# Threshold attention into a SwiGLU feed-forward: long score bursts from step 48, one last group of four chunks, and a feed-forward paced over 16 steps

## The chip, the cores and the metric

The kernel runs on one core of one Trainium2 chip. The metric is the device time of one execution in microseconds (us). Shown of the kernel before are four such times and one profiled execution. Engine names: PE is TensorE, DVE is VectorE, ACT is ScalarE, POOL is GpSimd, SP is SyncE, which here only issues DMAs.

## The reference, cut to what matters

Eight batches of eight heads, 576 positions, head width 64. Attention keeps only the scores within `tau` of the row's largest one; the result is the input of a gated feed-forward over 4608 rows of width 512, inner width 1536.

```python
scores = q @ k.T / 8
scores = where(scores >= max(scores, -1) - tau, scores, -1e9)
attn = exp(scores - max) / sum
x = (attn @ v) laid out as [8 * 576, 512]
xn = x / sqrt(mean(x * x) + 1e-6) * rms_g
out = (silu(xn @ w_gate) * (xn @ w_val)) @ w_out
```

## The kernel before

**Tiling.** The 4608 rows are 36 chunks of 128 rows: four main chunks for each batch, and one chunk (kind "v") for each pair of batches that holds their last 64 rows. A chunk takes four steps, one for each pair of heads, so there are 144 steps. In step s, PE computes 128 x 576 scores in fp32 for each of two heads into the two score tiles `s_ps` (two PSUM banks each; `emit_burst`, matmuls on L581). DVE moves them to `ssb` and takes the row extreme in the same instruction (L614, "TTR" below, with a small read of the accumulator after each). POOL makes the threshold (L652), ACT and partly POOL mask and exponentiate (L663 to L701), a DMA transposes the weights (L730), and PE multiplies them with V every second step (L748 and L753, "AV"). When a chunk's four steps are through, `emit_x` normalizes its 512 columns and a DMA transposes them into `xnT` (L800).

**Bursts.** A burst is one uninterrupted run of score matmuls. Up to step SB a burst is one step, 576 columns for each head. From step SB on a burst is 1024 columns for each head, both banks full, whatever step they belong to (`plan_bursts`); a step's scores are then cut in pieces at the ends of bursts, and each piece has its own TTR. A burst may begin when all TTRs of the burst before it have read the score banks. If a burst touches a "v" chunk, all of it is made of 64 x 64 matmuls.

**Feed-forward.** Chunks are collected in groups (SIZES); a group's rows are the moving columns, 256 for two chunks and 512 for four. `emit_ffn` makes 12 slices of the inner width: four gate matmuls (L854), four value matmuls (L859), a tanh on ACT (L868), two operations on DVE (L871, L876). Then 12 output matmuls for each chunk (L924), in two halves (OUT_PART), a move out of PSUM to `osb` (L937 on DVE or L939 on ACT, chosen by OUT_DVE) and a store on SP's queue (L944). The last group is "streamed": its output matmuls (L899) follow its gates slice by slice into accumulators that stay open, the banks named by ACC, and its moves out alternate between DVE and ACT.

**Order.** Nothing is ordered by hand. Every operation has an engine, a planned cost, a priority in units of steps and the operations that it needs. `order_ops` simulates the engines and, on each engine, picks what can start first, and among those the lowest priority; the program is then issued in that order, and each engine runs its list in order. A group's first slice has as priority the step of its last chunk plus LAG, or the end of the group before it, whichever is later, and its 12 slices are spread over PACE steps for each 512 columns; with SPREAD the output matmuls of its chunks follow, spread over as many steps again. PART_PRIO draws an output's second half forward. A move out of PSUM and a tanh stand 40 steps ahead of their slice (PUSH), so they go as soon as their input is there. A TTR of step s has priority s - 1 + TTR_PRIO.

**PSUM.** Four banks are a ring for everything but scores. After the last TTR the banks in OPENS join the ring.

Of the kernel before, what the change touches and what calls it, by code (L numbers as in the profile page):

```python
# [15 lines left out]
COST = dict(  # L16
    s_main=965.0, s_virt=960.0, tr_qk=530.0, tr4=230.0, tr_full=440.0, av_main=290.0, av_virt=370.0, ffn4=215.0, warm=3500.0,
    evac_qk=600.0, evac_qk_act=465.0, evac_half=252.0, evac_kt=330.0, evac_kt_act=252.0, prelu=667.0, exp2=1060.0, exp1=666.0, exp0=590.0,
    mask_d=680.0, mask_g=1810.0, take_g=1360.0, trw=510.0, evac_w=400.0, evac_wp=900.0, rz=210.0, xmul=341.0, sq=612.0, xn=773.0,
    pool_tiny=302.0, pool_mean=944.0, pool_dma=880.0, cast_v=620.0, cast_vt=475.0, cast_w=665.0,  # L20
    sp=420.0, sp_v=600.0, sp_w=600.0, sp_tr=1300.0, sp_qk=680.0, sp_tl=630.0,
)
# [105 lines left out]
def kernel(  # L128
# [14 lines left out]
    NT, DM = out.shape  # L143
# [11 lines left out]
    def sb(name, shape, dt=FP32):  # L155
        return konst.tile(shape, dt, tag=name, name=name)
# [25 lines left out]
    ssb = [sb(f"ssb{i}", [128, 2, S]) for i in range(3)]  # L182
# [22 lines left out]
    hf = [sb(f"hf{i}", [128, 512], FP16) for i in range(12)]  # L205
    hf += [stg.bitcast(FP16)[:, 512 * i:512 * (i + 1)] for i in range(NHF - 12)]
    osb = [sb(f"osb{i}", [128, DM]) for i in range(2)]

    s_ps = [ps(f"s_ps{h}", 1024) for h in range(2)]
    ROW_AT = 512 - S // 2  # L210
# [12 lines left out]
    def add(eng, cost, prio, deps, fn, **kw):  # L223
        o = Op(eng, cost, prio, deps, fn, **kw)
        ops.append(o)
        return o
# [57 lines left out]
    o_id, o_c, o_v, o_g = setup()  # L284
# [258 lines left out]
    ttr_of, exp_of, wt_of, av_of = {}, {}, {}, {}  # L543
# [23 lines left out]
    def emit_burst(segs, prio, runs):  # L567

        info = {s: parts_of(s) for s, _, _, _ in segs}
        no_whole = any(w is None for _, w, _ in info.values())  # L570
        deps = [x for d, _, _ in info.values() for x in d] + last_ttr
        made = []
        for run in runs:
            def fn(o, run=run):
                for s, lo, hi, at in run:
                    _, whole, quads = info[s]
                    p = steps[s][1]
                    for rows, i, lhs in quads if no_whole or o.quad else whole:
                        for h in range(2):
                            hs = HALF[h]  # L580
                            nc.tensor.matmul(s_ps[h][rows, at:at + hi - lo], lhs(hs), kT[i][p][h][hs, lo:hi],  # L581
                                             start=True, stop=True)

            n = sum(hi - lo for _, lo, hi, _ in run)
            o = add("PE", COST["s_main"] * n / S if not no_whole else COST["s_virt"] * n / S, prio if not made else -600.0,
                    deps + made[-1:], fn, mode=2 if no_whole else 1)
            if not made and REL_N[0] <= prio < REL_N[1]:
                o.release = REL[0] + REL[1] * prio
            made.append(o)
        for s in info:  # L590
            ci, p = steps[s]
            kind, b, c = chunks[ci]
            s_of.setdefault(s, made[0])
            if kind == "m":
                last_s.setdefault(("k", b, p), [])
                last_s["k", b, p] = last_s["k", b, p] + made
            else:
                last_sv[b, p] = last_sv.get((b, p), []) + made
                for e in range(2):
                    last_s.setdefault(("k", 2 * b + e, p), [])  # L600
                    last_s["k", 2 * b + e, p] = last_s["k", 2 * b + e, p] + made
        last_ttr.clear()
        for s, lo, hi, at in segs:
            first, last = lo == 0, hi == S
            if first:
                buf = s % 3
                held = exp_of[ssb_user[buf]] if buf in ssb_user else []
                ssb_user[buf] = s
            else:
                held = []  # L610
            for h in range(2):
                def ttr(o, s=s, lo=lo, hi=hi, at=at, h=h, first=first, last=last):
                    m = s % 6
                    nc.vector.tensor_tensor_reduce(  # L614
                        out=ssb_of(s)[:, h, lo:hi], in0=s_ps[h][:, at:at + hi - lo], in1=zrow[:, lo:hi],
                        scale=-1.0 / 8.0, scalar=3.0e38 if first else mxp[m][:, h:h + 1], op0=ALU.add, op1=ALU.min,
                        accum_out=(mx if last else mxp)[m][:, h:h + 1])

                before = [] if first else [ttr_of[s, h]]
                t = ttr_of[s, h] = add("DVE", 75.0 + (hi - lo) / 0.96, s - 1 + TTR_PRIO, made + [o_c] + held + before, ttr)  # L620
                last_ttr.append(t)

    last_ttr = []
# [204 lines left out]
    count = dict(hf=0, gv=0, o=0, v=[])  # L828
    clock = [0.0]

    def emit_ffn(slot, parts, ready_step, pace, streamed):

        n = 128 * len(parts)
# [4 lines left out]
        clock[0] = st + pace * n / 512.0  # L838
        xops = [t for _, t in parts]
        hs = []  # L840
        mm = 4 * (COST["ffn4"] if n == 512 else 112.0 if n == 256 else 60.0)
        el = n / 0.96 + 65.0
        uses = []
        for fc in range(NFC):
# [4 lines left out]
            hi = count["hf"] % NHF  # L849
# [28 lines left out]
            t = add("ACT", n / 1.2 + 49.0, pr - PUSH[0], [g, th_use.get(i)], tanh)  # L878
# [8 lines left out]
        if streamed:  # L887
# [6 lines left out]
            for n_, (fc, js) in enumerate(turns):  # L894
                hi, m_ = hs[fc]
# [16 lines left out]
        for j, (ci, _) in enumerate(parts):  # L912
            kind, b, c = chunks[ci]
            pr = st + dt * (NFC + (j + OUT_AT) * (NFC / len(parts) if SPREAD and not streamed else 1.0))
            oi = count["o"] % 2
            count["o"] += 1
            if streamed:
                mo, at = acc, j
            else:
                mo, at = None, 0  # L920
                for lo in range(0, NFC, OUT_PART):
                    def omm(o, j=j, lo=lo, first=mo):
                        for fc in range(lo, lo + OUT_PART):
                            nc.tensor.matmul(ring[(first or o).slot[0]], hf[hs[fc][0]][:, 128 * j:128 * (j + 1)],  # L924
                                             wo[:, fc], start=(fc == 0), stop=(fc == NFC - 1))

                    need = [m_ for _, m_ in hs[0:lo + OUT_PART]] + wo_ld + (outs[-1:] if mo else [])
                    o = add("PE", OUT_PART * COST["ffn4"], pr - (0.0 if lo == 0 else PART_PRIO), need, omm, ring=None if mo else "R")
                    mo = mo or o
                    outs.append(o)  # L930

            late = streamed and j % 2
            on_dve = streamed and not late or not streamed and OUT_DVE[ci % len(OUT_DVE)]

            def ev(o, oi=oi, mo=mo, at=at, on_dve=on_dve):
                if on_dve:
                    nc.vector.tensor_scalar(out=osb[oi], in0=ring[mo.slot[at]], scalar1=0.5, scalar2=None, op0=ALU.mult)  # L937
                else:
                    nc.scalar.activation(out=osb[oi], in_=ring[mo.slot[at]], func=AF.Copy, scale=0.5)  # L939

            def store(o, oi=oi, kind=kind, b=b, c=c, late=late):
                if kind == "m":
                    dst = out[b * S:b * S + MAIN].rearrange("(si sc) d -> si sc d", sc=4)[:, c]
                    (nc.scalar if late else nc.sync).dma_start(out=dst, in_=osb[oi])  # L944
                else:
                    for e in range(2):
                        r0 = (2 * b + e) * S + MAIN
                        nc.sync.dma_start(out=out[r0:r0 + TAIL], in_=osb[oi][64 * e:64 * e + 64])

            e = add("DVE" if on_dve else "ACT", 600.0 if on_dve else 476.0, pr - PUSH[0],  # L950
                    [last_out[j] if streamed else outs[-1], osb_use.get(oi)], ev,
                    frees=(mo, at))
            late = late and kind == "m"
            osb_use[oi] = add("ACT" if late else "SP", COST["sp"] if kind == "m" else 1100.0, pr, [e], store,
                              dma=DMA_NS['out'])
# [25 lines left out]
    n = 0  # L981
    for c in range(DFF // 512):
        for d in range(0, 4, 2):
            for w_dram, w_sb in ((moe_w_gate, wg), (moe_w_val, wv)):
# [7 lines left out]
                lo = gated(add("SP", COST["sp_w"], pr, w_use[slot], load, dma=2 * DMA_NS['w'], bulk=True), pr)  # L992
# [21 lines left out]
    for s, (ci, p) in enumerate(steps):  # L1014
# [6 lines left out]
        if p == NP - 1:  # L1021
            gi, j = place[ci]
# [23 lines left out]
            o.fn(o)  # L1046


PACE = 13.0
SQ_DVE = (0,)  # L1050
OUT_DVE = (0,)
LAGS = ()
SB = 64
TTR_PRIO = 1.0
BY_ROW = 4
ACC = (4, 6)
OPENS = ((4,), (6,))
NHF = 24
SPREAD = True
OUT_AT = 0.0  # L1060
PART_PRIO = 1.0
SIZES = (2, 2, 2, 2, 4, 4, 4, 4, 4, 4, 2, 2)
LAG = 16.0
LAT_TR = 3000.0
LAT_LD = 2000.0
REL = (0.0, 0.0)
# [64 lines left out]
```

## Time and profile before

| | us |
|---|---|
| median of 4 runs | 551.6 |
| lowest and highest | 550.87, 552.32 |
| profiled execution, its time | 552.32 |
| profiled execution, its span | 550.5 |
| PE busy in the span | 541.6 |
| ACT busy | 451.1 |
| DVE busy | 434.0 |
| POOL busy | 322.5 |

The profiled execution is the slowest of the four; 1.8 us of its time lie outside the span. A profile's row of a group gives the line, the engine, the operation, the tiles out<-in, the shape, the count, then busy time in us and the mean of one in ns, then the idle time ahead of it and what ended it. PE's matmuls overlap in the records, so the distance from one block's start to the next block's start is what counts, and a block in which a matmul waits shows as a longer busy block.

### The profile page before, as it was taken

What the parts mean: (1) busy time and instruction counts of PE and PEld (TensorE: products, weight loads), DVE (VectorE), ACT (ScalarE), POOL (GpSimd) and SP (SyncE); (2) the same over time, 40 slices, a digit from 0 to 9 for tenths busy, and PEclk for the clock granted to TensorE, in tenths of its full rate; (3) what the DMA queues carried; (4) which work ended last, traced back from release to release, by engine and by line L of the source; (5) the groups of instructions that cost most, each with busy time, mean ns of one, the idle gap of its engine ahead of it and who ended that gap; (6) DMA issues with size and microseconds to landing.
All of it is one profiled execution on the core that took longest, in us unless ns stands there. A gap on an engine that the chain in (4) does not pass through costs nothing.

```text
span 550.5 us, 15126 instructions
## 1 busy us (share of the span) xinstructions
PE 541.6 (98%) x5664; PEld 313.8 (57%) x5664; DVE 434.0 (79%) x1251; ACT 451.1 (82%) x741; POOL 322.5 (59%) x462
## 2 busy tenths in 40 slices
PE   8999999999999999999999999999999999999997
PEld 4656666666667455545555556555655454455764
DVE  4898988888878688878896889798897889775633
ACT  5898889899988889788989899899899988863332
POOL 2367846886777666665758467667767665631000
PEclk9999999999999999999999999999999999999999
DMA  8999999879998688798998698989997664740111
GB/s 194 246 274 280 170 179 215 162 128 186 188 194 178 132 172 157 161 188 167 176 206 159 116 200 179 198 153 214 188 180 152 127 123 94 157 95 29 40 58 57
DMA packets 270025, 89.07 MB, mean 162 GB/s; under 512 B 252544, under 2 KB 262272, under 8 KB 269952
## 3 DMA queue, kind: packets, MB, share of 16 engines
q1 hardware_dynamic: 267168, 86.02, 79.5%
q0 software_dynamic: 1600, 1.57, 1.9%
q8 instruction: 44, 0.72, 0.5%
q10 hardware_dynamic: 1184, 0.52, 0.3%
q14 instruction: 29, 0.24, 0.1%
HBM read 37.75 MB, written 9.44 MB: 86 GB/s over the span
## 4 chain that ended last, share of the span: by engine, by line
PE 90%; ACT 3%; DMA 2%; POOL 2%; DVE 2%; issue 1%; SPq 0%; DVEq 0%
PE s_ps L581 26%; PE ring L854 16%; PE ring L859 16%; PE ring L924 15%; PE ring L753 6%; PE ring L306 2%; PE ring L748 2%; DVE ssb L614 1%; DMA stg<-in_moe_w_val_dram 1%; PE s_ps L859 1%; PE s_ps L854 1%; ACT ssb L663 1%; DMA stg<-in_moe_w_gate_dram 1%; PE s_ps L899 1%; PE s_ps L924 1%
## 5 line engine op out<-in xcount | busy, mean ns | idle before, releaser
L614 DVE CUSTOM_DVE_ANT_0 ssb<-s_ps,zrow 128x576 f32<-128x576 f32 (+8 forms) x288 | 182.1, 669 | 26.0 <-PE s_ps L581 21.8
L663 ACT ACTIVATE ssb<-ssb,nth 128x576 f32<-128x576 f32 x224 | 166.6, 767 | 22.5 <-POOL nth L652 22.1
L581 PE MATMUL s_ps<-qkt 64*64 64x288 f32 (+16 forms) x1688 | 158.8, 415 | 2.3 <-DVE mx L614 1.8
L696 POOL TENSOR_SCALAR wsb<-ssb,nth 128x576 f16<-128x576 f32 x64 | 110.5, 1727 | 9.4 <-DMA wt<-wsb 2.6
L581 PEld LDWEIGHTS s_ps<-qkt 64*64 64x64 f32 (+1 forms) x1688 | 77.0, 144 | 60.0 <-issue 19.4
L854 PE MATMUL ring<-xnT,wg 128*128 128x256 f16 (+1 forms) x536 | 109.7, 327 | 0.2 <-DVE wt L724 0.2
L859 PE MATMUL ring<-xnT,wv 128*128 128x256 f16 (+1 forms) x536 | 109.7, 327 | 0.0
L670 ACT ACTIVATE wsb<-ssb 128x1152 f16<-128x1152 f32 x80 | 92.8, 1160 | 1.1
L652 POOL TENSOR_SCALAR nth<-mx 128x2 f32<-128x2 f32 x144 | 31.7, 220 | 105.5 <-DVE mx L614 91.0
L871 DVE SCALAR_TENSOR_TENSOR sl<-th,ring 128x512 f32<-128x512 f32 (+1 forms) x134 | 73.6, 551 | 25.1 <-ACT th L868 24.5
L701 POOL TENSOR_TENSOR wsb<-wsb,esb 128x576 f16<-128x576 f16 x64 | 81.9, 1280 | 9.5 <-ACT esb L682 5.0
L868 ACT ACTIVATE th<-ring 128x512 f32<-128x512 f32 (+1 forms) x134 | 64.3, 481 | 21.8 <-PE ring L854 18.1
L859 PEld LDWEIGHTS <-wv 128*128 128x128 f16 x576 | 53.0, 98 | 42.0 <-issue 8.7
L854 PEld LDWEIGHTS <-wg 128*128 128x128 f16 x576 | 53.2, 98 | 39.9 <-issue 6.7
L614 DVE CUSTOM_DVE_ANT_0 ssb<-s_ps,zrow,mxp 128x128 f32<-128x128 f32 (+7 forms) x80 | 38.2, 515 | 24.4 <-PE s_ps L581 24.0
L682 ACT ACTIVATE esb<-ssb,nth 128x576 f16<-128x576 f32 x64 | 49.3, 770 | 7.8 <-POOL nth L652 7.7
L753 PE MATMUL ring<-va,wt 128*128 128x65 f16 (+1 forms) x1280 | 50.9, 193 | 0.0
L924 PE MATMUL ring<-wo,hf 128*128 128x512 f16 x204 | 48.4, 380 | 0.0
L753 PEld LDWEIGHTS <-wt 128*128 128x128 f16 (+1 forms) x1280 | 46.1, 100 | 3.0
L667 ACT ACTIVATE wsb<-ssb 128x576 f16<-128x576 f32 x64 | 43.5, 680 | 1.1
L924 PE MATMUL ring<-wo,stg 128*128 128x512 f16 x180 | 42.2, 379 | 0.0
L876 DVE TENSOR_TENSOR hf<-ring,sl 128x512 f16<-128x512 f32 (+1 forms) x68 | 38.3, 564 | 4.0
(71 smaller groups left out, 566.1 us busy)
## 6 DMA issues: line engine op xcount, KB each, us to landing
vst<-in_v_dram SPq DMA_DIRECT2D x32, 256.0 KB, 3.6
qkn<-in_k_dram SPq DMA_DIRECT2D x31, 256.0 KB, 4.4
out_dram<-osb SPq DMA_DIRECT2D x31, 256.0 KB, 2.7
qkn<-in_q_dram SPq DMA_DIRECT2D x28, 256.0 KB, 4.5
stg<-in_moe_w_gate_dram SPq DMA_DIRECT2D x6, 512.0 KB, 6.2
stg<-in_moe_w_val_dram SPq DMA_DIRECT2D x6, 512.0 KB, 6.6
wt<-wsb SPq DMA_TRANSPOSE x128, 3.4
wo<-in_moe_w_out_dram POOLq DMA_DIRECT2D x4, 384.0 KB, 6.7
```

Source lines behind the costliest of these rows:

```text
L581: nc.tensor.matmul(s_ps[h][rows, at:at + hi - lo], lhs(hs), kT[i][p][h][hs, lo:hi], start=True, stop=True)
L614: nc.vector.tensor_tensor_reduce(out=ssb_of(s)[:, h, lo:hi], in0=s_ps[h][:, at:at + hi - lo], in1=zrow[:, lo:hi], scale=-1.0 / 8.0, scalar ...
L663: nc.scalar.activation(out=sb_[:, h], in_=sb_[:, h], func=PRELU, scale=-1.0, bias=nth[m][:, h:h + 1], **PRELU_KW)
L670: nc.scalar.activation(out=wsb[s % NW], in_=sb_, func=AF.Exp)
L696: nc.gpsimd.tensor_scalar(out=wsb[s % NW][:, h], in0=sb_[:, h], scalar1=nth[m][:, h:h + 1], scalar2=None, op0=ALU.is_le)
L701: nc.gpsimd.tensor_tensor(out=wsb[s % NW][:, h], in0=wsb[s % NW][:, h], in1=esb[es], op=ALU.mult)
L753: nc.tensor.matmul(ring[o.slot[0]][rs, at:at + D + 1], w[:, 5 * h + j, rs], va[vi][:, p, 2 * j + h], start=False, stop=(h == 1 and j == 3))
L854: nc.tensor.matmul(ring[o.slot[0]][:, 0:n], wg[d][:, fs], xnT[slot][:, d, 0:n], start=(d == 0), stop=(d == 3))
L859: nc.tensor.matmul(ring[o.slot[0]][:, 0:n], wv[d][:, fs], xnT[slot][:, d, 0:n], start=(d == 0), stop=(d == 3))
L868: nc.scalar.activation(out=th[i][:, 0:n], in_=ring[g.slot[0]][:, 0:n], func=AF.Tanh, scale=0.5)
L871: nc.vector.scalar_tensor_tensor(out=sl[i][:, 0:n], in0=th[i][:, 0:n], scalar=1.0, in1=ring[g.slot[0]][:, 0:n], op0=ALU.add, op1=ALU.mult)
L924: nc.tensor.matmul(ring[(first or o).slot[0]], hf[hs[fc][0]][:, 128 * j:128 * (j + 1)], wo[:, fc], start=(fc == 0), stop=(fc == NFC - 1))
```

## The change

- SB goes from 64 to 48: 16 steps more are done in bursts of 1024 columns.
- TTR_PRIO goes from 1.0 to 0.0 for all steps (TTR_FROM is 0, so TTR_EARLY is not used).
- The last two groups of two chunks become one of four. It is the streamed one, its four accumulators are the four score banks, and all four open after the last TTR of their head. Its third and fourth chunk move to buffers that lie on `ssb` instead of `osb`.
- OUT_DVE goes from 0 to 1: the move out of PSUM of the groups that are not streamed goes from ACT to DVE.
- PACE goes from 13 to 16, LAG from 16 to 12, PART_PRIO from 1 to 2.
- The planner's cost of a gate slice of 256 columns goes from 112 to 113 ns for each matmul; 512 columns keep 215.

```diff
+    osb += [ssb[0][:, 0, 0:DM], ssb[0][:, 0, 0:DM], ssb[1][:, 0, 0:DM], ssb[2][:, 0, 0:DM]]
...
-                t = ttr_of[s, h] = add("DVE", 75.0 + (hi - lo) / 0.96, s - 1 + TTR_PRIO, made + [o_c] + held + before, ttr)
+                t = ttr_of[s, h] = add("DVE", 75.0 + (hi - lo) / 0.96, s - 1 + (TTR_PRIO if s >= TTR_FROM else TTR_EARLY), made + [o_c] + held + before, ttr)
...
-        mm = 4 * (COST["ffn4"] if n == 512 else 112.0 if n == 256 else 60.0)
+        mm = 4 * {512: 215.0, 384: 189.0, 256: 113.0, 128: 60.0}[n]
...
-            oi = count["o"] % 2
+            oi = 2 + j if streamed and j > 1 else count["o"] % 2
...
-PACE = 13.0
+PACE = 16.0
 SQ_DVE = (0,)
-OUT_DVE = (0,)
+OUT_DVE = (1,)
 LAGS = ()
-SB = 64
-TTR_PRIO = 1.0
+SB = 48
+TTR_PRIO = 0.0
+TTR_EARLY = 1.0
+TTR_FROM = 0
 BY_ROW = 4
-ACC = (4, 6)
-OPENS = ((4,), (6,))
+ACC = (4, 5, 6, 7)
+OPENS = ((4, 5), (6, 7))
...
-PART_PRIO = 1.0
-SIZES = (2, 2, 2, 2, 4, 4, 4, 4, 4, 4, 2, 2)
-LAG = 16.0
+PART_PRIO = 2.0
+SIZES = (2, 2, 2, 2, 4, 4, 4, 4, 4, 4, 4)
+LAG = 12.0
```

## The prediction

> **What bounds the kernel now.** I read the page first. PE is busy nearly all the span, and the chain that ended last runs through it.
>
> ```profile
> PE 541.6 (98%) x5664; PEld 313.8 (57%) x5664; DVE 434.0 (79%) x1251; ACT 451.1 (82%) x741; POOL 322.5 (59%) x462
> PE 90%; ACT 3%; DMA 2%; POOL 2%; DVE 2%; issue 1%; SPq 0%; DVEq 0%
> ```
>
> A busy PE may hide waits, so next come the stages (columns: window, its length, then busy us of PE, weight loads, DVE, ACT, POOL, each with its count).
>
> ```profile
> 60.00:160.00 100.00, 99.83 (x1235) 65.41 (x1235) 83.34 (x237) 90.81 (x161) 71.35 (x98) 1.00 1.02 177
> 160.00:220.00 60.00, 60.00 (x657) 34.15 (x655) 49.16 (x127) 53.04 (x89) 38.53 (x55) 1.00 0.87 162
> 220.00:300.00 80.00, 79.67 (x798) 43.94 (x802) 65.84 (x202) 69.77 (x110) 53.17 (x71) 1.00 0.91 175
> 300.00:380.00 80.00, 80.00 (x847) 43.18 (x837) 67.92 (x209) 71.61 (x114) 52.83 (x73) 1.00 0.92 175
> 380.00:480.00 100.00, 100.00 (x1055) 52.13 (x1054) 84.03 (x264) 91.34 (x145) 68.53 (x93) 1.00 0.77 148
> ```
>
> From 60 to 480 us PE is full at a granted clock of 1.00, ACT is busy 376.6 of 420 us (89.7%) and DVE 350.3 (83.4%). Last I read the chain in order of time, start to start, for what a burst costs and where one waits.
>
> ```profile
> 144.91 1.57 PE s_ps L581 x16
> ...
> 148.92 1.13 PE s_ps L581 x16
> ...
> 154.09 1.80 PE s_ps L581 x16
> ...
> 225.79 1.89 PE s_ps L581 x32
> 227.68 0.97 PE ring L854 x4
> 228.65 0.86 PE ring L859 x4
> ```
>
> A short burst takes 1.13 us and a long one 1.89. The block next to a burst takes 0.97 where it otherwise takes 0.86: 0.11 for each burst. Blocks of 1.57 and 1.80 are short bursts that waited. In the PE timeline I found five such: at 55.9 (0.36 over), 59.3 (0.67), 144.8 (0.45), 154.0 (0.67) and, with transposes attached, 161.1 (0.67): 2.8 us. After 165 us every burst takes its plain time. So outside the first 60 us the change can take time only out of PE's own work, out of these 2.8 us, and out of the end.
>
> **The change, part by part.**
>
> *Long bursts from 48.* Sixteen steps are 16 short bursts, 16 x (1.13 + 0.11) = 19.8 us; in the long form 16 x 576 / 1024 = 9 bursts, 9 x (1.89 + 0.11) = 18.0. **Gain 1.8 us**, on PE, which is full there. DVE pays: 9 bursts cut 16 steps into 24 pieces, 16 TTRs more for two heads. A whole TTR is 753 ns; pieces of 448 and 128 columns are 620 + 349, and another accumulator read is 83: 0.3 us each, 4.8 us in all, beside PE's work. Steps 48 to 63 ran from 161 to 220 us, where DVE is busy 49 of 60. Without that cover it costs at most 4.8. That the "v" steps 52 to 55 now lie in long bursts costs nothing by the rows: long bursts with the later "v" steps also took 1.88 to 1.89.
>
> *One last group of four.* In the PE timeline four matmuls of 256 columns take 0.437 us and four of 512 columns 0.862. The two groups' 48 blocks of the first kind (21.0) become 24 of the second (20.7): **0.3 us** on PE. DVE saves 24 x (416 + 422) - 12 x (682 + 689) ns = 3.7 us, in the end phase, where it idles.
>
> *OUT_DVE.* The moves out of PSUM change engine.
>
> ```profile
> L939 ACT ACTIVATE osb<-ring 128x512 f32<-128x512 f32 x32 | 18.8, 588 | 15.1 <-PE ring L924 15.0
> ...
> 546.07 0.69 DVE L937 TENSOR_SCALAR osb<-s_ps 128x512 f32<-128x512 f32 x1 [0.80 <-PE s_ps L899]
> ```
>
> ACT had 35 of 36, DVE will have 34: ACT loses 33 x 0.59 = 19.5 us, DVE gains 33 x 0.69 = 22.8. Counted in the windows, 26 lie between 60 and 480 us: DVE there goes to 350.3 + 17.9 + 4.8 = 373 of 420 (88.8%), ACT to 376.6 - 15.3 = 361 (86.0%). The load is turned over, not raised beyond where ACT was. Behind a move on DVE stand TTRs, and PE's next burst waits for those; the move goes first by its priority. Cover: DVE sat idle 38.7 us between 80 and 480 waiting for a burst to end, so it usually had caught up; 22.7 us come off that, 16 stay. Cost between a gain (the TTR pair at 153.2 us started 1.54 us late, by the wait row because of ACT's `osb`, and the 1.80 burst follows) and 26 x 0.69 = 17.9 us. I take zero, the end next to the row: no burst after 165 us waited on an ACT as full as DVE will be.
>
> The Trainium skill speaks against this edit: "Advanced Engine Details and Errata", section on the read-write bubble, says that ScalarE is closer to PSUM and VectorE to SBUF, to be used accordingly. The two rows agree in direction, 0.59 against 0.69, and so by the rule the edit loses 3.3 us of engine time in 33 moves. By the stage table that is not time of the kernel, since neither engine is the one that is full.
>
> *TTR_PRIO.* TTRs go ahead of gate work that is due at the same time.
>
> ```profile
> 158.91 0.42 DVE L871 SCALAR_TENSOR_TENSOR sl<-th,ring 128x256 f32<-128x256 f32 x1 [0.90 <-ACT th L868]
> 159.43 0.42 DVE L876 TENSOR_TENSOR stg<-ring,sl 128x256 f16<-128x256 f32 x1
> 159.90 0.42 DVE L871 SCALAR_TENSOR_TENSOR sl<-th,ring 128x256 f32<-128x256 f32 x1
> 160.24 0.75 DVE L614 CUSTOM_DVE_ANT_0 ssb<-s_ps,zrow 128x576 f32<-128x576 f32 x1
> ```
>
> The burst at 157.84 ended at 158.97; its TTRs stood behind three gate operations, the first of which waited for ACT, until 160.24, and the burst at 161.05 waited 0.67. The others behave alike. All 2.8 us are of the kinds that this edit and the last act on. In return gate operations are later and hold ring banks longer. Gain between 2.8 us and a loss of the same size; **I take half, 1.4**, as a new order makes some waits of its own.
>
> *PACE, LAG, PART_PRIO.* The groups' work is moved, not changed. A group of four arrives every 16 steps; before, 13 steps of gates were followed by three without, now they are even. The first gate cannot come much sooner: the second `xnT` of the first group landed at 49.3 us and the first gate ran at 52.6. Stores on SP and moves on DVE go along with the outputs, in the same number. I take zero, between a gain of 3.3 us (all of that distance) and the seam below.
>
> *The seam.* Before, the last burst began at 478.1 and ended at 479.9; the last `xnT` landed at 500.9, 20.9 us later, and 27 us went by before PE used it, with other groups' work. Now the last group needs all its four chunks first. What else is left? Before, two of the next-to-last full group's slices were done when the last burst began, by due time a cut at step 145. The same cut leaves now: of the group due from 139, seven of 12 slices (7 x 1.72 = 12.1 us) and its outputs (4 x 2.59 = 10.4), two outputs of the one before it (5.2), and three AVs (1.8): 29.5 us against 20.9. **Nothing lost**, with 8.6 us to spare. At the very end, slices of 512 columns need 0.7 us more from gate to product (0.584 + 0.682 + 0.689 against 0.375 + 0.416 + 0.422), but outputs run about five slices behind, and the last move and store stay as they are.
>
> **Sum.** 1.8 + 0.3 + 1.4 = 3.5 us. The profiled execution took 552.3 (span 550.5 and 1.8 around it), which gives 548.8; it stands 0.7 above the median, so for the median of runs I say 551.6 - 3.5 = **548.1**.
>
> **Rivals.**
> 1. *DVE becomes late for the bursts* (slower). Place: 160 to 480 us, TTRs behind moves out of PSUM. For it: DVE at 88.8%, and the moves come first. Against it: 16 us of waiting for PE remain. It decides the sign once PE loses over 3.5 us, that is six bursts in 54 by 0.67 each. If every other of the 26 moves costs its 0.69, 9.0 us: 551.6 - 3.5 + 9.0 = 557.1; with a third 554.1.
> 2. *The last group starves PE at the seam* (slower). If PE runs ahead of its due times by six more steps (some 4 slices and an output, 9.5 us), the spare 8.6 is gone; each step further costs about 2 us. With three: 548.1 + 6 = 554.
> 3. *The gain is given back*: TTRs and moves trade waits, PE loses in new places the 1.4 and the 1.8; 551.6, that is, the change does not do what it is to do.
> 4. *More*: all five waits go (1.4 more), and the slices move up into the start by 1 us: 545.7.
>
> **How the numbers follow.** Forecast 0.57, with 546.5 to 550.4 about it; rival 4 0.11; rival 3 0.10; rival 1 0.13; rival 2 0.09. The bound for same is 0.2%, 1.1 us, about what a measurement of this kernel can tell from no change. Faster 0.57 + 0.11 = 0.68, same 0.10, slower 0.22. For 8 in 10 I take the forecast, rivals 3 and 4 and the near edge of the slower ones: 545.3 to 553.0.
>
> **What would show it.** Right: 54 bursts of 1.89 us and 48 short ones; 24 last blocks of 0.86; short bursts of 1.13 between 140 and 165 us or none there; PE full from the last burst to the last output; DVE near 89% and ACT near 86% in the loaded stretch. Wrong: long bursts over 1.9 us or PE idle ahead of them, released by DVE (rival 1); PE idle some 20 us after the last burst, released by `xnT` (rival 2). The prediction falls if the planner's new order lets DVE fall behind its plan, which I can't see in this trace.

## The result, and the profile after

The changed kernel takes 552.95 us (median of 38 runs, 551.36 to 554.78), the kernel before on the same chips 551.98 (60 runs, 550.69 to 554.15): ratio 1.0018, 95% interval 1.0012 to 1.0024. It is slower by about 1.0 us; I had forecast 3.5 us less than 551.6, that is 548.1. The four runs shown of before had their median 0.4 us under the one of the 60, so 0.4 us of the difference to my number is only that. Of all executions in this document one, of the rows kernel below, took 1361 us; it is left out of every number.

First the page of the profiled execution (time 551.96 us, span 550.2): engines, the chain by engine, and two groups of section 5.

```profile
PE 538.4 (98%) x5556; PEld 304.1 (55%) x5556; DVE 454.5 (83%) x1292; ACT 434.0 (79%) x696; POOL 322.1 (59%) x462
...
PE 86%; DMA 3%; DVE 3%; ACT 3%; POOL 2%; issue 1%; SPq 1%; ACTq 0%; POOLq 0%; DVEq 0%
...
L582 PE MATMUL s_ps<-qkt 64*64 64x288 f32 (+17 forms) x1676 | 155.8, 414 | 1.2 <-DVE mx L615 0.8
...
L855 PE MATMUL ring<-xnT,wg 128*128 128x512 f16 (+1 forms) x496 | 107.1, 338 | 1.6 <-DVE qkt L454 1.1
```

PE is busy 3.2 us less than before, near the 3.5 of the forecast, yet the span hardly moved, as PE is idle 2.9 us more; its share of the chain fell from 90% to 86%, and those of DVE and DMA rose from 2% to 3% each. The last column says for what PE sat idle. New there are the gate blocks (L855) that wait for a copy of DVE (L454). The row of the bursts (L582, 0.8 us on score reads) says nothing about the loaded stretch: its two waits lie at 32.8 and 41.4 us, and the five such waits of the kernel before (1.8 us) all lie in the first 51 us. For the loaded stretch the length of a burst tells, start to start; three lines of the chain of the kernel after, in order of time:

```profile
175.38 1.89 PE s_ps L582 x32
...
308.24 1.89 PE s_ps L582 x32
...
423.75 1.89 PE s_ps L582 x24
```

Of the 54 long bursts 53 take 1.82 to 1.95 us, as the 45 long ones of before do; one, at 168.6 us, takes 2.16, which is 0.3 more than its kind. The old waits at 144.8, 154.0 and 161.1 us are gone. So rival 1, bursts late because of DVE, didn't come. The stages of the kernel after, in the columns of the prediction's table:

```profile
60.00:160.00 100.00, 99.85 (x1227) 65.96 (x1225) 86.94 (x241) 88.00 (x156) 68.77 (x93) 1.00 1.01 176
160.00:220.00 60.00, 59.30 (x642) 34.51 (x640) 53.18 (x159) 51.22 (x85) 38.32 (x55) 1.00 0.84 160
220.00:300.00 80.00, 79.52 (x797) 43.22 (x794) 68.52 (x209) 67.29 (x104) 53.07 (x72) 1.00 0.94 181
300.00:380.00 80.00, 79.66 (x835) 42.77 (x834) 71.80 (x215) 69.59 (x109) 53.32 (x73) 1.00 0.90 167
380.00:480.00 100.00, 100.00 (x1054) 52.37 (x1051) 87.72 (x267) 85.78 (x134) 66.81 (x91) 1.00 0.79 142
```

DVE does 368.2 of 420 us (I had said 373) and ACT 361.9 (361). The granted clock is 1.00 as before. What I had not said is the third column: PE is no longer full from 160 to 380 us (59.30, 79.52 and 79.66 us, before 60.00, 79.67 and 80.00). The PE timeline shows where (start, duration, then the idle time before and what ended it):

```profile
208.96 0.22 PE L749 MATMUL ring<-va,wt 128*128 128x130 f16 x1
...
210.34 1.02 PE L855 MATMUL ring<-xnT,wg 128*128 128x512 f16 x4 [0.63 <-DVE qkt L454]
...
265.69 1.02 PE L855 MATMUL ring<-xnT,wg 128*128 128x512 f16 x4 [0.48 <-DVE qkt L454]
...
338.89 0.46 PE L307 MATMUL ring<-id,qkn 64*128 64x64 f32 x8 [0.34 <-DMA qkn<-in_q_dram]
...
542.95 1.89 PE L900 MATMUL s_ps<-wo,hf 128*128 128x512 f16 x8 [0.78 <-DVE osb L938]
545.62 0.81 PE L900 MATMUL s_ps<-wo,hf 128*128 128x512 f16 x3 [0.78 <-DVE ssb L938]
```

Two kinds matter. After an AV block, a gate block finds no free ring bank: the bank was still to be copied by DVE. And at the very end two of the streamed group's output rows wait for DVE's move out of the row before. The starts of neighbouring matmuls show the full price of such a wait: 0.95 us each at the end, 0.79 and 0.65 at 210 and 265.

**The account.** Both kernels stream the same number of columns in all, so I summed over the trace, for each matmul, the distance to the next start beyond its streaming time (0.42 ns a column of f16, by the blocks of 0.862 and 0.437 us in the prediction; 0.84 ns a column of f32 for the two or four matmuls that run side by side, by neighbouring starts in a burst), and set the two kernels against each other by which block follows which. From 80 us on the kernel after has +2.1 us among output blocks (the end), +2.0 from AVs to gate blocks (the ring: 0.79, 0.65 and, at 497.6 us, 0.35; the rest in small amounts), +0.7 among transposes (they wait for a load of `qkn`), and -3.0 in bursts and the blocks next to them: 1.8 us of old waits gone, and 1.2 because there are fewer changes into and out of bursts. That is +1.8. In two more profiles of the unchanged kernel after it is +2.1 and +2.4, in a second one of before 0.0. In the first 80 us the sum is 23.0 to 23.7 after and 24.2 and 25.3 before, some 1.4 less. Spans agree: 550.2, 550.8 and 551.4 after, 550.5 and 549.4 before, on the mean +0.8, beside +1.0 by the medians. The pair of profiles in the prediction and above happened to be a long execution of before and a short one of after.

### The profile page after: what moved, and what is told of

Its sections match the earlier page's. It is cut to its first block, busy times and chain, and to the rows that moved or that the text cites. A ratio compares the mean times of both kernels' runs of the same rounds, so it can differ in the third digit from the quotient of the medians.

```text
span 550.2 us, 14896 instructions
## 1 busy us (share of the span) xinstructions
PE 538.4 (98%) x5556; PEld 304.1 (55%) x5556; DVE 454.5 (83%) x1292; ACT 434.0 (79%) x696; POOL 322.1 (59%) x462
## 4 chain that ended last, share of the span: by engine, by line
PE 86%; DMA 3%; DVE 3%; ACT 3%; POOL 2%; issue 1%; SPq 1%; ACTq 0%; POOLq 0%; DVEq 0%
PE s_ps L582 26%; PE ring L855 16%; PE ring L860 16%; PE ring L925 13%; PE ring L754 5%; PE s_ps L900 2%; DVE ssb L615 2%; PE ring L307 2%; PE ring L749 2%; DMA qkn<-in_q_dram 2%; PE s_ps L925 1%; PE s_ps L855 1%; DMA stg<-in_moe_w_gate_dram 1%; ACT ssb L664 1%; PE s_ps L860 1%
## 5 line engine op out<-in xcount | busy, mean ns | idle before, releaser
L615 DVE CUSTOM_DVE_ANT_0 ssb<-s_ps,zrow 128x576 f32<-128x576 f32 (+8 forms) x288 | 176.7, 652 | 10.7 <-PE s_ps L582 9.5
L582 PE MATMUL s_ps<-qkt 64*64 64x288 f32 (+17 forms) x1676 | 155.8, 414 | 1.2 <-DVE mx L615 0.8
L860 PE MATMUL ring<-xnT,wv 128*128 128x512 f16 (+1 forms) x508 | 110.1, 339 | 0.2 <-ACT qTv L476 0.2
L582 PEld LDWEIGHTS s_ps<-qkt 64*64 64x64 f32 (+1 forms) x1676 | 77.1, 144 | 58.5 <-issue 24.0
L855 PE MATMUL ring<-xnT,wg 128*128 128x512 f16 (+1 forms) x496 | 107.1, 338 | 1.6 <-DVE qkt L454 1.1
L872 DVE SCALAR_TENSOR_TENSOR sl<-th,ring 128x512 f32<-128x512 f32 (+1 forms) x124 | 71.5, 578 | 8.3 <-ACT th L869 7.7
L855 PEld LDWEIGHTS <-wg 128*128 128x128 f16 x528 | 47.7, 98 | 45.6 <-issue 10.6
L860 PEld LDWEIGHTS <-wv 128*128 128x128 f16 x528 | 48.6, 98 | 41.4 <-issue 4.9
L615 DVE CUSTOM_DVE_ANT_0 ssb<-s_ps,zrow,mxp 128x128 f32<-128x128 f32 (+7 forms) x96 | 45.8, 515 | 23.1 <-PE s_ps L582 22.5
L683 ACT ACTIVATE esb<-ssb,nth 128x576 f16<-128x576 f32 x64 | 49.3, 770 | 11.6 <-POOL nth L653 11.4
L877 DVE TENSOR_TENSOR hf<-ring,sl 128x512 f16<-128x512 f32 (+1 forms) x69 | 41.0, 596 | 6.7 <-PE ring L860 2.5
L925 PE MATMUL ring<-wo,hf 128*128 128x512 f16 x168 | 39.4, 380 | 0.0
```

The lines of the kernel that those rows point to most:

```text
L615: nc.vector.tensor_tensor_reduce(out=ssb_of(s)[:, h, lo:hi], in0=s_ps[h][:, at:at + hi - lo], in1=zrow[:, lo:hi], scale=-1.0 / 8.0, scalar ...
L855: nc.tensor.matmul(ring[o.slot[0]][:, 0:n], wg[d][:, fs], xnT[slot][:, d, 0:n], start=(d == 0), stop=(d == 3))
L860: nc.tensor.matmul(ring[o.slot[0]][:, 0:n], wv[d][:, fs], xnT[slot][:, d, 0:n], start=(d == 0), stop=(d == 3))
L872: nc.vector.scalar_tensor_tensor(out=sl[i][:, 0:n], in0=th[i][:, 0:n], scalar=1.0, in1=ring[g.slot[0]][:, 0:n], op0=ALU.add, op1=ALU.mult)
```

## The experiments

The theory: the gain came, and new waits took it back, in the ring after score reads that now go first, and at the end. Rivals: DVE's load as such; each part of the change costs something of its own; less work in reserve between scores because of LAG and PACE (C); any re-plan of this order costs about as much (D). The letters A and B are defined anew in each expectation below. All ratios are against the kernel before, run beside it on the same chip; where the text says only how many us slower or faster a kernel is, that is worked out from the ratios, and the interval is 0.6 to 1.0 us to either side. A wait "of 0.95" is the distance between starts beyond the usual one.

| kernel | ratio [95%] | span of its profile |
|---|---|---|
| after + rows of the end spread ("the rows kernel") | 1.0006 [0.9993, 1.0019] | 549.6 |
| the same, second time | 1.0005 [0.9992, 1.0019] | 551.6 |
| after, second time | 1.0016 [1.0004, 1.0028] | 550.8 |
| after, third time | 1.0018 [1.0004, 1.0031] | 551.4 |
| before, second time | 1.0003 [0.9989, 1.0016] | 549.4 |
| before + SB 48 | 1.0024 [1.0014, 1.0035] | 551.6 |
| before + last group of four | 1.0052 [1.0034, 1.0069] | 552.8 |
| before + OUT_DVE 1 | 1.0028 [1.0015, 1.0040] | 552.8 |
| before + moves on DVE, order held | 1.0021 [1.0008, 1.0034] | 551.7 |
| before + TTR_PRIO 0 | 1.0042 [1.0028, 1.0057] | 554.3 |
| before + PACE, LAG, PART_PRIO | 1.0065 [1.0052, 1.0079] | 552.9 |
| before + planner's cost 113 | 1.0025 [1.0011, 1.0039] | 551.2 |
| rows + TTR_PRIO 1.0 | 1.0112 [1.0094, 1.0129] | 557.4 |
| rows + TTR_PRIO 0.5 | 1.0054 [1.0038, 1.0070] | 553.8 |
| rows + SB 64 | 1.0032 [1.0018, 1.0046] | 551.6 |
| rows + key-tail copy all on ACT | 1.0021 [1.0006, 1.0036] | 551.4 |
| rows + key-tail copy moved forward | 1.0022 [1.0009, 1.0034] | 551.1 |
| rows + moves on ACT, order held | 1.0001 [0.9987, 1.0015] | 549.5 |

### The end: rows of one tile

The order of the program shows the cause of the waits at the end. Banks 4 and 5 lie in one score tile, `s_ps_163`, and banks 6 and 7 in the other; the rows of the streamed group take them in this order. In the kernel after (each line a matmul of L900, in PE's order):

```
L900 Matmult s_ps_163<-wo,hf_160 128x512
L900 Matmult s_ps_163<-wo,hf_157 128x512
L900 Matmult s_ps_163<-wo,hf_158 128x512 [waits DVE_49]
```

The third line belongs to the second row, in its own bank, and waits until DVE has moved the first row out of the other bank of that tile. (The kernel before had its two accumulators in banks 4 and 6, one in each tile.) The Trainium skill ("PSUM — Partial Sum Buffer", section "The four PSUM rules") says that each bank is a separate physical SRAM, which speaks for a wait that the program asks for, not the chip; no run here gives each bank a tile of its own. The experiment gives neighbouring rows different tiles and leaves the order alone.

```diff
     seq = order_ops(...)
+    for o in seq:
+        if o.pick:
+            o.slot = [4, 6, 5, 7]
```

> The changed kernel; only the order of the four open accumulators is permuted, so that the last four rows of output matmuls alternate between the two score tiles. Theory A (the gain was made and given back at the end, where the second row waits for the move out of the first because both lie in one tile): the two idle stretches of 0.78 us, 0.95 us start to start each, shrink to 0.2 or less, PE ends 1.5 to 1.9 us sooner, the time is 551.1 to 551.5 where the changed kernel has 552.95. Rival B (the loss is DVE's load in the loaded stretch): the end is off the account, 552.5 to 553.

Measured beside it, on the same chip, the unchanged kernel after:

> The changed kernel once more, for a second profile: the first profile's execution (551.96) lay 1 us under the median of its kernel. If the median's surplus is waits that differ from run to run, this profile has the same blocks of PE's own work and other or longer waits in the loaded stretch; theory A says the two waits of 0.95 us at the end are in it again, rival B that the stretch from 160 to 480 us has more waits on DVE. Time 552.5 to 553.4.

552.47 us against 553.11, 0.64 less. The timeline of PE at the end, from the last 12 matmuls of the group before, in the kernel after:

```profile
537.47 2.75 PE L925 MATMUL ring<-wo,stg 128*128 128x512 f16 x12
540.06 2.11 PE L900 MATMUL s_ps<-wo,hf 128*128 128x512 f16 x9
```

(its other two lines stand above), and PE and ACT in the rows kernel:

```profile
538.15 2.75 PE L925 MATMUL ring<-wo,stg 128*128 128x512 f16 x12
540.74 4.56 PE L900 MATMUL s_ps<-wo,hf 128*128 128x512 f16 x20
```

```profile
545.34 0.60 ACT L940 ACTIVATE osb<-s_ps 128x512 f32<-128x512 f32 x1 [8.12 <-PE s_ps L900]
545.83 0.59 ACT L940 ACTIVATE ssb<-s_ps 128x512 f32<-128x512 f32 x1
```

The 20 output matmuls now run through: both waits are gone, so their cause is shown. They take PE 4.56 us instead of 6.37 (540.06 to 546.43), 1.8 less. Of that 1.3 reaches the start of the last move (545.83, 5.09 us after the first of the 20; in the kernel after 546.46, 6.40 after it), and 1.2 the end of the span. The second row's move on ACT, whose data were ready about 1.7 us earlier (the row ended two rows of 0.86 before), waits until the fourth row, in the same tile, is through, and then the last move stands behind it. And 0.2 us are lost again before: the first streamed outputs now wait for DVE once more, in both profiles of the rows kernel and in none of the kernel after:

```profile
519.38 0.81 PE L900 MATMUL s_ps<-wo,hf 128*128 128x512 f16 x3 [0.19 <-DVE hf L877]
```

From the last matmul of the last burst to the end of the span it is 68.15 or 68.16 us in three profiles of the kernel after, 67.14 and 67.15 in two of the rows kernel: 1.0 us is what the shared tile costs this kernel. My expectation of 1.5 us and more took PE's waits for the kernel's time.

> The rows kernel of the first experiment once more, beside the change and before on one chip. If the two rows in one tile cost what the two waits at the end show, it takes 1.2 to 1.9 us less than the change of this call; if the first comparison (0.64 less) was the whole of it, 0.4 to 0.8 less.

551.78 us against 553.61, 1.8 less; by the ratios the two comparisons give 0.6 and 0.7 us. The medians of a dozen runs scatter by as much as the effect, so they don't decide between the two; the 1.0 us of the traces lies between them.

> The kernel before with the last two groups of two made one of four in four open banks, and nothing else. Theory A: 0.3 us less of PE's work and two waits of 0.95 us at the end, so 1.6 us more: 553.6 (553.2 to 554.0). Rival B: 551.4 to 552.0, the waits at the end are not part of it.

```diff
+    osb += [ssb[0][:, 0, 0:DM], ssb[0][:, 0, 0:DM], ssb[1][:, 0, 0:DM], ssb[2][:, 0, 0:DM]]
...
+            oi = 2 + j if streamed and j > 1 else count["o"] % 2
...
+ACC = (4, 5, 6, 7)
+OPENS = ((4, 5), (6, 7))
...
+SIZES = (2, 2, 2, 2, 4, 4, 4, 4, 4, 4, 4)
```

The last group of four alone costs 0.52%, 2.9 us (interval 1.9 to 3.8), more than I expected. Its plan is that of before until the end, and its timeline has three waits of 0.95, one at 511.4 us, in an output block that waits for DVE (L877), and two at the end (the last group's rows again):

```profile
545.76 1.89 PE L900 MATMUL s_ps<-wo,hf 128*128 128x512 f16 x8 [0.78 <-DVE osb L938]
548.43 0.81 PE L900 MATMUL s_ps<-wo,hf 128*128 128x512 f16 x3 [0.78 <-DVE ssb L938]
```

Three times 0.95 less the 0.3 us that PE saves is 2.55; from the last burst to the end of the span its profile is 2.5 us longer than that of before.

### The parts alone

> The kernel before with long bursts from step 48 and nothing else. Theory A: the term stands, 102 bursts in place of 109, 1.8 us less of PE's work, 550.2 (549.8 to 550.6). Rival B, 16 more pieces for DVE, with the stretch already at 82% on DVE: 551.5 to 552.5.

```diff
-SB = 64
+SB = 48
```

1.3 us slower instead of faster. Nine new waits stand in its timeline, 0.2 to 1.0 us each, between 150 and 265 us, about 4 us in all, most of them for DVE or ACT ahead of AV, gate and value blocks; the gain of the longer bursts is smaller than these.

> The kernel before with the moves out of PSUM on DVE (OUT_DVE 1) and nothing else. Theory A (what the change lost is two waits at the end and three waits for ring banks that come from the new order, not DVE's load as such): within 0.8 us of the kernel before, DVE near 88% and ACT near 86% in the loaded stretch, no burst after 170 us longer than plain. Rival B (DVE's load): 2 us or more above the kernel before, with PE waits released by DVE spread over 160 to 480 us.

```diff
-OUT_DVE = (0,)
+OUT_DVE = (1,)
```

1.5 us slower. From 60 to 480 us DVE is busy 363.6 us and ACT 360.3; waits of 1.3 and 1.4 us came ahead of blocks that start at 164.6 and 175.4 us.

> The kernel before with TTR_PRIO 0 and nothing else. Theory A: the waits of short bursts at 144, 154 and 161 us shrink from 1.8 us to under 0.9, and blocks that take a ring bank wait in their place, 0.5 to 0.8 us each, behind a DVE move that now stands after two TTRs; the two about cancel: 0.5 us under to 1 us above the kernel before. Rival B, that TTRs first is plain gain: 1.5 to 2.5 us under it.

```diff
-TTR_PRIO = 1.0
+TTR_PRIO = 0.0
```

2.3 us slower. The old waits at 143, 152 and 159 us stayed, which I had put to this edit. New ones of 0.6 and 0.8 us came at 253 and 258 us; the largest new one is a pair of transposes behind late loads:

```profile
332.67 0.46 PE L306 MATMUL ring<-id,qkn 64*128 64x64 f32 x8 [1.23 <-DMA qkn<-in_k_dram]
333.60 0.63 PE L306 MATMUL ring<-id,qkn 64*128 64x64 f32 x8 [0.47 <-DMA qkn<-in_q_dram]
```

> The kernel before with PACE 16, LAG 12, PART_PRIO 2 and nothing else. Theory A: only the order of feed-forward work moves, 0.8 us either way of the kernel before. Rival C (less feed-forward work in reserve lets PE wait more): 1 to 3 us above it, with waits in the loaded stretch or PE idle some 20 us after the last burst.

```diff
-PACE = 13.0
+PACE = 16.0
...
-PART_PRIO = 1.0
+PART_PRIO = 2.0
...
-LAG = 16.0
+LAG = 12.0
```

3.6 us slower, the dearest part, which I had at zero. By due time the small groups now end at step 51 and the first group of four is due from 59. Before there was such a gap too, from 53.5 to 63, but PE came to it later: the last slice of 256 columns ran at 179.3 us there and runs at 170.3 here, while the first of 512 columns runs at 187.3 instead of 189.5. In between PE has no gates. Two bursts then follow one another with nothing between, and PE can only wait for the reads:

```profile
182.70 1.87 PE L581 MATMUL s_ps<-qkt,qTv 64*64 64x288 f32 x16 [0.26 <-DVE mx L614]
185.54 1.87 PE L581 MATMUL s_ps<-qkt,qTv 64*64 64x288 f32 x16 [0.97 <-DVE mx L614]
187.35 1.04 PE L854 MATMUL ring<-xnT,wg 128*128 128x512 f16 x4
```

The place fits rival C; which of the three settings does it, no run tells. The five runs of parts alone sum to 1.3 + 2.9 + 1.5 + 2.3 + 3.6 = 11.6 us; together the edits cost 1.0. They are not terms of a sum.

> The kernel before with only the planner's cost of a gate matmul of 256 columns at 113 ns instead of 112, the one edit that I priced at nothing without a word. No instruction changes, only their order. Theory D (the order before is one that a search picked, and any new order adds some us of waits): 1 to 4 us above the kernel before, with one to four waits of 0.4 us or more that it does not have. Theory A (waits come from what each edit does): within 0.5 us.

```diff
-        mm = 4 * (COST["ffn4"] if n == 512 else 112.0 if n == 256 else 60.0)
+        mm = 4 * (COST["ffn4"] if n == 512 else 113.0 if n == 256 else 60.0)
```

One nanosecond in the planner's cost, which changes nothing but the order, costs 1.4 us. The old waits stay, and new ones of 0.6, 0.2 and 0.5 us came at 263, 264 and 293 us. Rival D holds as far as it goes: the size of a re-plan is the size of this change's result. It is one other plan, so it does not say that every one costs that. But every part alone was re-planned too, so its cost is that of the edit and of a new order together.

### What works only together

> The changed kernel with the four rows alternating between the tiles, as in the run before, and TTR_PRIO back at 1. Theory A: the waits for ring banks at 209 and 265 us (0.8 and 0.65 us) are gone, as the moves that free the banks no longer stand behind two TTRs; waits of bursts in the first 165 us come back, 0.5 to 1.8 us; the time is within 0.7 us of the alternating kernel. Rival B (DVE's load): as many waits as with TTR_PRIO 0, at other places.

```diff
-TTR_PRIO = 0.0
+TTR_PRIO = 1.0
```

With the old TTR_PRIO the rows kernel takes 1.1% more than before, 5.9 us more than with the new one, where alone the new value cost 2.3. The place is the gap without gates again:

```profile
182.72 0.85 PE L582 MATMUL s_ps<-qkt 64*64 64x256 f32 x5 [1.39 <-DVE mxp L615]
...
187.71 2.61 PE L582 MATMUL s_ps<-qkt,qTv 64*64 64x384 f32 x26 [2.63 <-DVE mxp L615]
```

This is rival 1 as I described it, held off in the change by reads that go first. The other half of the expectation failed. The waits for ring banks did not go; AV blocks now wait for the same copy, and on DVE three reads of the burst still stand ahead of it:

```profile
218.05 0.22 PE L749 MATMUL ring<-va,wt 128*128 128x130 f16 x1 [0.55 <-DVE qkt L454]
272.21 0.22 PE L749 MATMUL ring<-va,wt 128*128 128x130 f16 x1 [0.60 <-DVE qkt L454]
```

And the old waits of bursts between 140 and 165 us did not come back: every burst there takes 1.07 to 1.13 us. So neither the new waits nor the lost ones belong to TTR_PRIO alone.

> The rows kernel with score reads half a step less early (TTR_PRIO 0.5 instead of 0.0), re-planned. If the reads going first are what holds the ring banks at 209 and 265 us and the bursts can bear half a step, both waits go and it takes 0.5 to 1.5 us less than the rows kernel. If, as with TTR_PRIO 1.0 inside the change (5.8 us more), the bursts then wait for DVE, it takes 1 to 4 us more.

```diff
-TTR_PRIO = 0.0
+TTR_PRIO = 0.5
```

Half a step costs 2.7 us over the rows kernel. The gate block's wait at 210 us is gone, but an AV at 215 waits 0.87 us for the same copy (L454) and one at 269 us 0.45, and more waits came at 171, 225 and 262 us.

> The changed kernel with alternating rows and SB back at 64. With LAG 12 and PACE 16 the groups of two end at step 51 by due time and the first group of four starts at 59, so in between PE has little but scores. Theory E (long bursts from 48 are what carries that gap): the short bursts from step 51 on wait for their TTRs as they do in the kernel with the pace alone (2.7 us there), 2.5 to 5 us above the alternating kernel. If the burst's own cost is all: 1.8 us above.

```diff
-SB = 48
+SB = 64
```

1.5 us slower than the rows kernel, near the 1.8 that I had worked out for the bursts' own cost and short of theory E. It is no clean measure of the bursts, as this is another plan; the gap without gates takes part of it:

```profile
182.96 1.87 PE L582 MATMUL s_ps<-qkt,qTv 64*64 64x288 f32 x16 [0.87 <-DVE mx L615]
```

### The ring at 210 and 265 us

DVE's timeline in the kernel after shows what the gate block at 210.34 waited for. The burst ended at 207.3, and four score reads stood ahead of the copy that frees the bank:

```profile
207.45 0.55 DVE L615 CUSTOM_DVE_ANT_0 ssb<-s_ps,zrow,mxp 128x320 f32<-128x320 f32 x1 [0.22 <-PE s_ps L582]
...
209.07 0.76 DVE L615 CUSTOM_DVE_ANT_0 ssb<-s_ps,zrow 128x576 f32<-128x576 f32 x1
209.75 0.08 DVE L615 DVE_READ_ACCUMULATOR2_ANT mx<- 128x1 f32 x1
209.86 0.43 DVE L454 COPY qkt<-ring 64x256 f32<-64x256 f32 x1
```

> The changed kernel with alternating rows, its order kept, and the second half of the move of a key tail issued on ACT instead of DVE, so that the ring bank is freed without standing behind two TTRs. If those two stand behind the waits of 0.8 and 0.65 us at 209 and 265 us, both go: 1.0 to 1.4 us under the alternating kernel, which makes 551.0 to 551.5 where the kernel before has 552.3, a little faster than it. If something else holds the bank, no change.

```diff
-                copy = nc.vector.tensor_copy if h else nc.scalar.copy
+                copy = nc.scalar.copy
```

The expectation failed: the waits grew to 1.15 and 1.05 us. On ACT the copy stood at 211.5 us, behind the exponentials of its own queue.

> The change with the rows of the end spread over the tiles (as in the first experiment), and DVE's half of the key-tail copy issued right after ACT's half instead of behind the two or more score reads that stood between them; nothing else in the order moves. If those reads in front of the copy hold the ring bank that the gate blocks at 209 and 265 us wait for, both waits (0.79 and 0.65 us) go and the kernel takes 1.0 to 1.4 us less than the rows kernel of the same call. If the bank is held by ACT's half, which has to come first, the waits stay and the time is that of the rows kernel within 0.4 us.

```diff
+    for x in [o for o in seq if o.eng == "DVE" and len(o.deps) == 2 and id(o.deps[1]) in tails]:
+        seq.remove(x)
+        seq.insert(seq.index(x.deps[1]) + 1, x)
```

`tails` holds ACT's half of each key-tail copy. Again no gain, 0.9 us more than the rows kernel by the ratio. But the timelines tell why. PE:

```profile
210.96 1.03 PE L857 MATMUL ring<-xnT,wg 128*128 128x512 f16 x4
212.43 1.02 PE L862 MATMUL ring<-xnT,wv 128*128 128x512 f16 x4 [0.44 <-DVE xsb L774]
```

and DVE:

```profile
209.92 0.43 DVE L455 COPY qkt<-ring 64x256 f32<-64x256 f32 x1
210.38 0.76 DVE L617 CUSTOM_DVE_ANT_0 ssb<-s_ps,zrow 128x576 f32<-128x576 f32 x1
...
211.74 0.18 DVE L773 RECIPROCAL rz<-ring 128x4 f32<-128x4 f32 x1
211.95 0.42 DVE L774 TENSOR_TENSOR xsb<-ring,rz 128x256 f32<-128x256 f32 x1
```

The gate block (here L857) runs without a wait, so the copy behind the reads was what held its bank. The next block needs the bank that the AVs filled, which DVE frees after the same reads: the wait went on, 0.60 instead of 0.79. Two bursts whose reads now come later waited in turn, at 142 and 386 us. In that stretch DVE's queue after a burst is what PE waits for; a single operation moved in it only passes the wait on.

### DVE's load by itself

> The kernel before with its order kept to the instruction, and the moves out of PSUM of the groups that are not streamed issued on DVE at the same place of the program (the planner still counts them as ACT's). Against the run with OUT_DVE 1 re-planned (2.2 us above) it tells DVE's load from the new order. Theory D: within 0.8 us of the kernel before, though DVE is as full as there. Rival B (DVE's load): 1.5 to 2.5 us above.

```diff
-                if on_dve:
+                if on_dve or not streamed:
```

The order of before is kept and only the engine of the moves changed: 1.2 us slower, between the two expectations. From 60 to 480 us DVE and ACT are both busy 365 us. Block by block against before, PE waits longer at four places: ahead of or among transposes at 163 and 276 us (0.6 and 0.4; those at 163 for a load of `qkn`), at an output block at 409 (0.3) and at a burst at 474 (0.2). Only the last of these is a burst, so a fuller DVE does not make bursts late here.

> The rows kernel with its planned order kept; only the moves out of PSUM of the groups that are not streamed are issued on ACT instead of DVE, 32 moves, so DVE has some 22 us less and ACT some 19 us more. If DVE's load as such costs what the mirrored kernel on before showed (about 1.0 us), it takes 0.7 to 1.2 us less than the rows kernel (about 551.0 to 551.8 where before is 552.0). If the waits come from the score reads going first and not from the moves, the waits at 209 and 265 us stay (no move stands near them) and the time is that of the rows kernel within 0.4 us. If moves late on an ACT that was planned without them hold ring banks, it takes 0.5 us or more longer.

```diff
-                if on_dve:
+                if on_dve and streamed:
```

The mirror of it, in the rows kernel: the first number after PE's pairs below is DVE's, now 352, and ACT's 373.

```profile
60.00:480.00 420.00, 418.30 (x4545) 238.82 (x4543) 351.92 (x1065) 373.27 (x609) 281.05 (x381) 1.00 0.89 165
```

It gains 0.2 to 0.3 us by the ratios, within their intervals, and the waits at 210 and 265 us stay, to 0.01 us:

```profile
210.77 1.02 PE L855 MATMUL ring<-xnT,wg 128*128 128x512 f16 x4 [0.63 <-DVE qkt L454]
```

So 16 us of load off DVE don't touch the ring's waits: they come from the order of DVE's queue (score reads ahead of the copy), not from its load, and DVE's load as such explains at most a small part. The wait at 498 us, which was for a move of an output, shrinks from 0.35 to 0.25.

### What differs from one execution to another

> The kernel before, unchanged, as a second profile. If its medians and its profiled execution differ by chance alone, the time is the same as before, ratio within 0.1% of 1, and the five old waits (55.9, 59.3, 144.8, 154.0, 161.1 us) come at the same places with the same sizes within 0.1 us.

> The change, unchanged, as a third profile. If the account of the first profile (the gain of some 3.3 us arrived, new waits of about 5 us) is no accident of one execution, the waits at 209, 265, 336, 543 and 546 us come again within 0.2 us, and the median stands 0.7 to 1.5 us over before.

Before, unchanged, is at 1.0003, the change at 1.0018. Of the five old waits that I had counted, the three at 144, 153 and 160 us came again, 1 us earlier; the two at 55.9 and 59.3 did not: they belonged to one execution. In the kernel after the waits at 210, 265, 339, 498 us and the end came again in every profile, their sizes within 0.2 us.

## Why the prediction was wrong, step by step

What failed is the end of the last group, which I took as unchanged, the reasons for the 1.4 us of TTR_PRIO, and the zero for PACE, LAG and PART_PRIO; behind all three, that parts of one plan can be priced one by one.

- **Long bursts from 48, 1.8 us.** Held inside the change: 1.5 us by taking it out, and in the account 1.2 us beside the old waits, with the new 0.3 us of the burst at 168.6 already taken off. Alone the edit is 1.3 us slower. My price without cover, at most 4.8 us, was for DVE's extra pieces; what came were waits of AV, gate and value blocks in a new order.
- **One last group of four, 0.3 us: failed.** The step that failed is "the last move and store stay as they are". I looked at the way from gate to product and not at which rows share a tile: two waits of 0.95 us on PE, 1.0 us of the kernel's time by the traces when the rows are spread (0.6 and 0.7 by the ratios).
- **TTR_PRIO, 1.4 us of 2.8: failed in its reasons.** I put all five old waits to this edit and the last one, and took the middle against a loss at ring banks. The three old waits after 80 us (1.8 us) are gone in the change, but this edit alone leaves them, and they don't return when it is taken back inside the change; the other 1.0 of my 2.8 did not come again in the second profile of before. The ring's new waits are 0.79 and 0.65 us behind score reads, and I had named the loss, but with TTR_PRIO back at 1 AV blocks wait for the same copy (0.55 and 0.60 us idle). The operations held back were not gate operations but copies of key tails and the AVs' own reads. What this edit does in the change is another thing: it holds off the waits of bursts at 183 and 188 us (1.39 and 2.63 us idle without it), which stood in my rival 1 but in no term.
- **OUT_DVE, zero.** Nearly right inside the change (0.2 to 0.3 us, within the intervals), 1.2 alone with the order held. The rule of the Trainium skill that I weighed ("Advanced Engine Details and Errata", "The Read-Write Bubble", ScalarE for PSUM) agrees in direction: all four comparisons have the moves on DVE as the slower.
- **PACE, LAG, PART_PRIO, zero: failed as a step.** Alone it is 3.6 us slower. In the change the same gap, from 173.7 to 183.7 us between gates, costs little, and with the reads later (TTR_PRIO 1) or the bursts short (SB 64) bursts wait in it.
- **The seam.** Right: in the last stretch of the profile after, PE waits only at the end and once for 0.35 us at 497.6.
- **The loads.** I named no price for DMAs of `qkn`; 0.7 us of transposes wait for them at 339 us.
- **The sum.** From 80 us on I had about -3.0 (1.8 + 0.3 + half of the 1.8 that lies there), measured is +2.1 over before's first profile. The difference of 5.1 is for the most part the end (2.1), the ring (2.0) and the transposes (0.7). The first 80 us gave some 1.4; what of it is the change I can't say, as two executions of one kernel differ there by 1.1.

What came is rival 3, the gain given back in new places, and a little more, though the part at the end is not the trade of reads and moves that I had named. I had given it 0.10, on the thought that a new order makes "some waits of its own", and priced those at 1.4 us. **Open** are four things: how the banks of key tails and AVs can be freed in time after a burst, why the loads of `qkn` come late at 339 us, what a version with one tile for each of the four rows gives (not tried), and whether a plan exists with the gain and without the waits. No version here beats the kernel before; the rows kernel, with either engine for the moves, stands equal with it.

## What to carry to other kernels

Where a planner orders the whole program, price an edit with the cost of a re-plan (here 1.4 us for one nanosecond in a cost) and don't add up terms that work only together. Where an engine's queue holds a run of long operations, here the score reads after a burst, ask what stands behind the run and frees a buffer for the engine that is full. At the end of a kernel, look at which accumulators share a tile: there a wait for a move out has no other work to cover it, and what PE gains back still has to pass the moves behind it.

## What of the hardware was not expected

Nothing in the chip's own rates: in the profiles of before and of the change the granted clock was 0.998 to 1.00, and instructions took their durations of before (a move on DVE 690 ns, on ACT 588 to 597). New to me was how much of a profile belongs to one execution: waits of 0.4 to 0.8 us in the first 60 us come and go (once, in the rows kernel, one of 1.5), and spans of one unchanged kernel lay between 550.2 and 551.4.
